# Holding operations behind transfers to program order from the third batch on, second buffers for q and k, and a sum as GpSimd's first library instruction

## The chip, the cores and the metric

The kernel runs on one core of a Trainium2 chip. The metric is the device time of one execution in microseconds (us); lower is better. A change within 0.2% (about 2.5 us) can't be told from no change.

## The reference, cut to what matters

```python
scores = scale * q @ k.T                                   # q, k, v: 8 batches, 8 heads, 576 x 64; scale = 1/8
bias   = -(cum[:, :, :, None] - cum[:, :, None, :])        # cum = cumsum of max(s, 0) along the 576
scores = where(causal, -1e9, scores + minimum(bias, 0))
attn   = exp(scores - max);  attn /= sum(attn) + 1e-9
x      = (attn @ v) with heads side by side                # 4608 tokens x 512
out    = (sigmoid(x @ w_gate) * (x @ w_val)) @ w_out       # w_gate, w_val: 512 x 1536, w_out: 1536 x 512
```

q, k and v are float32; the three weight matrices arrive as 64-bit floats and are decoded on the chip (`decode_weight`: three operations on VectorE and one on ScalarE for each block of 128 columns).

## The kernel before, in words

**Ticks.** 64 heads are gone through one after the other, each in five ticks: head `i`, tick `t` (0 to 4), `n = 5 i + t`. A tick takes one of five row blocks of the causal scores. The first eight heads (batch 0, functions `n_...`) work in float32; from head 8 on q, k, v and the probabilities are split into a high and a low half-precision part.

**What one head from head 8 on needs**, with the names that the profile uses:

- Every second head `load_qk` loads q and k of a pair of heads into `qk32` (queue SP), `qk_square` sums their squares (ScalarE, tile `jq`), a GpSimd all-reduce makes `qkt`, and `qk_scale` makes a power of two of it (`qksc`, `qkcf`; VectorE).
- `split_qk(i)`: two ScalarE operations write the high parts (L340, L342), two VectorE operations the low parts (L341, L343) into `qk16`, and one transposing transfer on SP (L345) turns it into the tile `T`. `swap_k(i)`: two more transfers on SP (L350, L351) copy the halves of k crosswise into `T[:, 2]`.
- `load_crow` fetches a row of cumulated biases from memory into `cr`, and GpSimd broadcasts it over the partitions. VectorE scales it to `rl`, GpSimd masks it (L403).
- `s_part(i, t)`: for each of six score pieces two matmuls on TensorE, the first (L388) against `T[:, 0]`, the second (L389) against the swapped copy `T[:, 2]`. Pieces are called `s46_4_0` (head 46, block 4, columns from 0), blocks go from 4 down to 0. `max_part` (L413, VectorE, tile `em`) adds bias and takes the maximum, ScalarE does the exponential (L416), `p_part` splits the probabilities (L420 ScalarE, L421 VectorE), a transposing transfer (`pt`) turns them, and two heads later `av_part` does 45 matmuls (L436 to L438).
- `v_square` loads a batch's v in four pieces on GpSimd's queue and sums squares on ScalarE for the batch after.

**FFN units.** 216 units (`gv`, 24 or 48 matmuls, L583; then `th` on ScalarE, `t` on VectorE, `h` on both; then six matmuls L613 into `o`) are dealt out over the ticks, each batch's units while the next batch is in attention; `m = n - 7` sets how far behind.

**What sets the order.** The code says what depends on what and a priority (the order in which it is written). A scheduler that goes by its own costs then fixes one order for each engine and each queue before the launch. On the chip every engine and every queue takes its instructions in that order, and one that waits holds up all behind it. `tc.keep_in_program_order(x)` places `x` behind everything that was written earlier for its engine.

**Buffers.** `qk32` and `qk16` have one buffer each, `T` two, `gv` (PSUM) two, the score banks three. The 24 tiles `t2f` (256 columns each) hold the first two FFN groups' results until the output weights are there; after tick 87 nothing uses them.

**GpSimd's sets of operations.** In GpSimd's order a row `ISA` without tiles (in the trace a `MODIFY_POOL_CONFIG`) stands where it is switched to another set of operations, called a library here; the profile of before has GpSimd idle behind both of them.

Of the kernel before, what the change touches and what calls it, by code (L numbers as in the profile page):

```python
# [7 lines left out]
F16 = mybir.dt.float16  # L8
# [15 lines left out]
def tile_attention_then_gated_ffn(  # L24
# [56 lines left out]
    for t, (q0, m, w) in enumerate(TILES):  # L81
# [7 lines left out]
    nc.gpsimd.memset(junk, 0.0)  # L89
    nc.gpsimd.affine_select(junk, junk, pattern=[[-1, P]], compare_op=ALU.is_ge, fill=0.0, base=0,  # L90
                            channel_multiplier=1)
    nc.vector.memset(ident, 0.0)
# [55 lines left out]
    sv = {}  # L148
    vss = {}

    def v_square(b, c):
        if c == 0:
            vss[b] = wp.tile([P, vch], F32, tag="vss", name=f"vss{b}")
        t = wp.tile([P, S], F32, tag="rl", name=f"vsq{b}_{c}")
        nc.gpsimd.dma_start(t, vview[b, c])
        nc.scalar.activation(t, t, AF.Square, accum_out=vss[b][:, c : c + 1])

# [49 lines left out]
    def load_weight(n):  # L207
# [3 lines left out]
        for x, src in enumerate((w_out,) if o else (w_gate, w_val)):  # L211
# [122 lines left out]
    def split_qk(i):  # L334
        p, j = divmod(i, 2)
        sc = qkc[p][0]
        t16 = wp.tile([QP, 2, QC, 2, D], F16, tag="qk16", name=f"qk16_{i}", bufs=1)
        q_ = qk32[p][:, 0, j]
        k_ = qk32[p][:, 1, j]
        nc.scalar.activation(t16[:, 1, :, 0], q_, AF.Copy, scale=sc[:QP, 0:1])  # L340
        nc.vector.scalar_tensor_tensor(t16[:, 1, :, 1], q_, sc[:QP, 0:1], t16[:, 1, :, 0], ALU.mult, ALU.subtract)  # L341
# [7 lines left out]
    def swap_k(i):  # L349
        nc.sync.dma_start(T[i][0:64, 2], T[i][64:128, 0])  # L350
        nc.sync.dma_start(T[i][64:128, 2], T[i][0:64, 0])  # L351

    def load_crow(i):
        crow[i] = wp.tile([P, S], F32, tag="cr", name=f"cr{i}")
        if i > 0:
            nc.sync.dma_start(crow[i][0:1], cum_d[i : i + 1, :])
        nc.gpsimd.partition_broadcast(crow[i], crow[i][0:1] if i > 0 else rel[0:1])  # L357

# [289 lines left out]
    nticks = NTL * NH  # L648
    for n in range(nticks + 8):
        i, t = divmod(n, NTL)  # L650
# [43 lines left out]
        if i < NH:  # L694
            p, j = divmod(i, 2)
            b, h = divmod(i, H)
            if t == 0 and i + 1 < NH:
                load_crow(i + 1)
            if i + 2 < NN:
                if j == 0 and t == 1:  # L700
                    n_load(p + 1)
                    load_v(p + 1)
                if j == 1 and t == 2:
                    with first():
                        n_prep(p + 1)
            elif i < NN:
                if j == 0:
                    if t == 2:
                        load_qk(p + 1)
                        load_v(p + 1)  # L710
                    if t == 4:
                        qk_square(p + 1)
            elif j == 0:
# [89 lines left out]
```

## Time and profile before

| | |
|---|---|
| three timed runs | 1224.86, 1225.04, 1225.22 us; median 1225.04 |
| the profiled execution | 1222.6 us; its span 1220.9 us |
| TensorE (PE) | busy 1114.0 us, 91% of the span |
| VectorE (DVE), ScalarE (ACT), GpSimd (POOL) | busy 783.0, 756.7, 299.4 us |
| granted TensorE clock, mean | 0.979 |

Busy is the time in which an engine had an instruction under way; matmuls overlap, so the share of PE is read as an upper bound. Rows of a timeline give start, duration, engine, line, tiles, and in brackets the idle time before with the instruction that ended it. SPq is the queue that SyncE feeds. A "lead" below is the PE work that stands between two instructions in the order. Head 18 begins at 273.7 us, head 63 at 1030.1 us.

### The profile page before, as it was taken

To read this page: it belongs to the slowest core of one execution; us is meant where nothing else is said; L and a number is where in the kernel's file an instruction comes from. 1 tells how busy PE (TensorE), PEld (TensorE's weight loads), DVE (VectorE), ACT (ScalarE), POOL (GpSimd) and SP (SyncE) were. 2 spreads that over 40 slices of the span, in tenths; PEclk is the share of its full clock that TensorE was granted. 3 is DMA by queue.
4 is the path that set the end of the run, shared out by engine and by line. 5 is a ranking of instruction groups with operands and counts; after the bars stand their busy time and mean duration, and the time that the engine had idled before them with its cause. 6 is when DMAs were issued, how large, how long until landed. Compare 5 with 4: busy or idle time off the path is not lost.

```text
span 1220.9 us, 30743 instructions
## 1 busy us (share of the span) xinstructions
PE 1114.0 (91%) x11924; PEld 871.3 (71%) x11924; DVE 783.0 (64%) x2194; ACT 756.7 (62%) x1505; POOL 299.4 (25%) x605
## 2 busy tenths in 40 slices
PE   2878687999999899999999999999999999999997
PEld 1666576667777777777777776777777777787774
DVE  4898997975777667764575566776677676422221
ACT  3988886766676667664665566676676676333222
POOL 2642543332232223221121122322232221000000
PEclk9976999999999999999999999999999999999999
DMA  8754798786786878783756477787888856300000
GB/s 226 213 154 133 173 199 169 150 162 130 153 153 135 152 135 155 157 164 70 130 113 128 80 151 150 149 145 158 149 156 143 168 103 122 55 19 10 10 18 18
DMA packets 464177, 157.51 MB, mean 129 GB/s; under 512 B 438495, under 2 KB 457951, under 8 KB 464030
## 3 DMA queue, kind: packets, MB, share of 16 engines
q1 hardware_dynamic: 444190, 117.79, 52.4%
q0 software_dynamic: 5440, 18.88, 5.0%
q10 hardware_dynamic: 14400, 18.88, 5.0%
q8 instruction: 93, 1.52, 0.5%
q14 instruction: 54, 0.44, 0.1%
HBM read 56.92 MB, written 9.58 MB: 54 GB/s over the span
## 4 chain that ended last, share of the span: by engine, by line
PE 34%; issue 24%; DMA 18%; DVE 9%; ACT 8%; POOL 4%; SPq 1%; POOLq 0%; ACTq 0%; DVEq 0%
PE gv L583 17%; DMA T<-qk 10%; PE o L613 9%; DMA qk<-in_q_dram 3%; DVE e L413 3%; DMA cr<-cum_d 2%; PE s L388 1%; PE na_ps L531 1%; ACT jq L313 1%; PE s L389 1%; PE s L502 1%; DMA vsq<-in_v_dram 1%; POOL cr L357 1%; ACT qk L340 1%; POOL rl L403 1%
## 5 line engine op out<-in xcount | busy, mean ns | idle before, releaser
L583 PE MATMUL gv<-x,w 128*128 128x256 f16 (+3 forms) x6912 | 618.7, 247 | 13.6 <-DVE t L590 9.9
L583 PEld LDWEIGHTS <-w 128*128 128x128 f16 x6912 | 536.2, 98 | 70.5 <-issue 15.9
L613 PE MATMUL o<-w2all,h 128*128 128x512 f16 x1296 | 314.1, 379 | 1.4 <-ACT osb L620 1.4
L403 POOL TENSOR_SCALAR_AFFINE_SELECT rl<-rl 128x64 f32<-128x64 f32 (+1 forms) x280 | 130.3, 466 | 380.1 <-DVE em L413 192.4
L416 ACT ACTIVATE e<-e,em 128x576 f32<-128x576 f32 x280 | 155.4, 557 | 75.3 <-DVE em L413 72.1
L613 PEld LDWEIGHTS <-h 128*128 128x128 f16 x1296 | 123.4, 98 | 108.8 <-issue 2.0
L590 DVE SCALAR_TENSOR_TENSOR t<-th,gv 128x256 f32<-128x256 f32 x192 | 80.0, 417 | 162.3 <-ACT th L588 162.2
L588 ACT ACTIVATE th<-gv,scb 128x256 f32<-128x256 f32 (+3 forms) x288 | 110.3, 408 | 114.9 <-PE gv L583 114.5
L598 ACT ACTIVATE h<-t,hsc 128x256 f16<-128x256 f32 x192 | 96.9, 505 | 92.0 <-DVE t L590 91.7
L421 DVE SCALAR_TENSOR_TENSOR p<-e,p 128x1152 f16<-128x1152 f32 x112 | 130.7, 1167 | 28.2 <-ACT p L420 27.6
L413 DVE CUSTOM_DVE_ANT_0 e<-s,rl,qkcf 128x288 f32<-128x288 f32 x280 | 134.5, 484 | 19.4 <-PE s L389 8.9
L599 DVE SCALAR_TENSOR_TENSOR h<-t,hsc,h 128x256 f16<-128x256 f32 x192 | 93.8, 488 | 41.3 <-ACT h L598 38.7
L420 ACT ACTIVATE p<-e 128x1152 f16<-128x1152 f32 x112 | 111.8, 998 | 3.7 <-DMA pt<-p 1.5
L388 PE MATMUL s<-T 128*128 128x288 f16 x336 | 86.7, 277 | 29.2 <-DVE em L413 25.8
L341 DVE SCALAR_TENSOR_TENSOR qk<-qk,qksc,qk 96x384 f16<-96x384 f32 x56 | 36.1, 645 | 87.9 <-ACT qk L340 87.8
L436 PE MATMUL av<-v,pt 128*128 128x65 f16 x840 | 84.5, 192 | 6.6 <-DMA pt<-p 6.4
L389 PE MATMUL s<-T 128*128 128x288 f16 x336 | 86.0, 277 | 3.4 <-DMA T<-T 3.4
L340 ACT ACTIVATE qk<-qk,qksc 96x384 f16<-96x384 f32 x56 | 34.3, 613 | 84.3 <-DMA T<-qk 83.8
L436 PEld LDWEIGHTS <-pt 128*128 128x128 f16 x840 | 77.2, 98 | 13.1 <-DMA pt<-p 7.7
L437 PE MATMUL av<-v,pt 128*128 128x64 f16 x840 | 84.4, 192 | 0.0
L438 PE MATMUL av<-v,pt 128*128 128x65 f16 x840 | 84.1, 194 | 0.0
L357 POOL PARTITION_BROADCAST cr<-cr x63 | 63.7, 1014 | 80.5 <-DMA cr<-cum_d 79.7
(149 smaller groups left out, 1305.0 us busy)
## 6 DMA issues: line engine op xcount, KB each, us to landing
vsq<-in_v_dram POOLq DMA_DIRECT2D x32, 288.0 KB, 4.1
out_dram<-osb POOLq DMA_DIRECT2D x36, 256.0 KB, 3.3
v<-in_v_dram SPq DMA_DIRECT2D x64, 128.0 KB
qk<-in_q_dram SPq DMA_DIRECT2D x28, 288.0 KB
qk<-in_k_dram SPq DMA_DIRECT2D x28, 288.0 KB
T<-T SPq DMA_DIRECT2D x112, 72.0 KB
ws<-in_moe_w_out_dram ACTq DMA_DIRECT2D x12, 512.0 KB
w2all<-in_moe_w_gate_dram ACTq DMA_DIRECT2D x8, 512.0 KB
```

The source lines that it names most:

```text
L388: nc.tensor.matmul(ps[:, : b_ - a], lhs, T[i][:, 0, a:b_], start=True, stop=False)
L389: nc.tensor.matmul(ps[:, : b_ - a], lhs, T[i][:, 2, a:b_], start=False, stop=True)
L403: nc.gpsimd.affine_select(rl[i][:, q0:w], rl[i][:, q0:w], pattern=[[-1, m]], compare_op=ALU.is_ge, fill=-MASKED if i < NN else MASKED, bas ...
L413: nc.vector.tensor_tensor_reduce(e_t[t][:, a:b_], ps[:, : b_ - a], rl[i][:, a:b_], c, init, ALU.add, ALU.min, acc)
L416: nc.scalar.activation(e_t[t][:, :w], e_t[t][:, :w], AF.Exp, bias=init, scale=-1.0)
L420: nc.scalar.activation(p_s[h_][:, 0], e_s[h_], AF.Copy, scale=PSCALE)
L421: nc.vector.scalar_tensor_tensor(p_s[h_][:, 1], e_s[h_], PSCALE, p_s[h_][:, 0], ALU.mult, ALU.subtract)
L436: nc.tensor.matmul(AV[i][:, t], hi, v_[:, D : 2 * D + 1], start=kb == 0, stop=False)
L583: nc.tensor.matmul(ps[:, gv, a:e], w1[f][:, cc, gv, wl], x_of(b, cc)[:, xl, c0 + a : c0 + e], start=(c == 0), stop=(c == 3 * NC - 1))
L588: nc.scalar.activation(th[:, a:e], ps[:, 0, a:e], AF.Tanh, scale=scb[b][:, f : f + 1])
L598: nc.scalar.activation(h[:, 0], t2, AF.Copy, scale=hsc[:, f : f + 1])
L613: nc.tensor.matmul(ps[:m], h[:, hl, tt * P : tt * P + m], w2[f][:, wl], start=(f == 0 and c == 0), stop=(f == NF - 1 and c == 2))
```

## The change

Six things, all in the order or the buffers; the arithmetic is the same.

1. GpSimd's first library instruction at the start, a mask on a scratch tile, becomes a sum over partitions.
2. The loads of weight blocks 0 and 1 go to the queue SP, written ahead of the first `cr` and v; block 2 stays on ScalarE's queue, held to program order.
3. From tick 90 (`more_room`; head 18) `spare` gives a second buffer for `qk32` (odd pairs) and for `qk16` (odd heads), both in the `t2f` tiles, now one tile.
4. From then on `pin` holds these behind all that is written before: the squares of q and k, `qk_scale`'s first operation, the first operation of `split_qk`, the two transfers of `swap_k`, the broadcast of `cr`, the sum of squares of v.
5. From then on they are written later: broadcast at tick 2 (was 0); q and k are loaded a pair of heads further ahead; squares at tick 0 of the odd head (was 4 of the even one), `qk_scale` at its tick 1 (was 0), `split_qk` of an even head at its tick 2 (was 1); `swap_k` of an even head at tick 4 (was 3). `v_square` loads a head earlier, the sum two ticks after its load.
6. From tick 110 on FFN units are dealt out nine ticks behind, not seven.

```diff
-    nc.gpsimd.affine_select(junk, junk, pattern=[[-1, P]], compare_op=ALU.is_ge, fill=0.0, base=0,
-                            channel_multiplier=1)
+    nc.gpsimd.partition_all_reduce(junk[:, 1:2], junk[:, 0:1], P, ADD_REDUCE)
...
+    def pin(ins):
+        return tc.keep_in_program_order(ins) if spare else ins
...
-    t2first = [cp.tile([P, GT], F32, name=f"t2f_{u}") for u in range(2 * NF)]
+    t2big = cp.tile([P, 2 * NF * GT], F32, name="t2f")
+    t2first = [t2big[:, u * GT : (u + 1) * GT] for u in range(2 * NF)]
+    spare = {}
+    def more_room():
+        c = 0
+        for name, n in (("qk16", QC * 2 * D), ("qk32", 4 * QC * D)):
+            spare[name] = t2big[:, c : c + n]
+            c += n
...
-            nc.scalar.dma_start(dst, src)
+            if n < 2:
+                nc.sync.dma_start(dst, src)
+            else:
+                d = nc.scalar.dma_start(dst, src)
+                if n == 2:
+                    tc.keep_in_program_order(d)
...
-        nc.scalar.activation(t16[:, 1, :, 0], q_, AF.Copy, scale=sc[:QP, 0:1])
+        pin(nc.scalar.activation(t16[:, 1, :, 0], q_, AF.Copy, scale=sc[:QP, 0:1]))
...
-        nc.sync.dma_start(T[i][0:64, 2], T[i][64:128, 0])
-        nc.sync.dma_start(T[i][64:128, 2], T[i][0:64, 0])
+        pin(nc.sync.dma_start(T[i][0:64, 2], T[i][64:128, 0]))
+        pin(nc.sync.dma_start(T[i][64:128, 2], T[i][0:64, 0]))
...
+            if t == (2 if spare else 0) and i + 1 < NH:
+                spread_crow(i + 1)
...
+                late = 1 if spare else 0
+                if t == 0 and p + 1 not in qkc:
                     qk_square(p + 1)
-            if NN - 1 <= i and j == 1 and i + 1 < NH:
-                if t == 0:
+                if t == late:
                     qk_scale(p + 1)
-                if t == 1:
+                if t == 1 + late:
                     split_qk(i + 1)
-            if t == 3 and NN - 1 <= i and i + 1 < NH:
+                if t == 3 and spare and i + 3 < NH:
+                    load_qk(p + 2)
+            if t == (3 + j if spare else 3) and NN - 1 <= i and i + 1 < NH:
                 swap_k(i + 1)
...
-        m = n - 7
+        m = n - (9 if n > 2 * NTL * H + 30 else 7)
```

How the order moves, at three places. First GpSimd's start, before (`ISA` without tiles: a library; `nq`: zeroed tiles of batch 0; `cr0`: the first broadcast):

```order
L362 MEMSET v32_0_168 64x130
L90 ISA
L90 AFFINE_SELECT scrap_89<-scrap_89 128x128
L479 MEMSET nq0_0_174 64x576
L479 MEMSET nq1_0_408 64x576
L479 MEMSET nq0_1_175 64x576
L479 MEMSET nq1_1_409 64x576
L362 MEMSET v32_1_261 64x130
L364 MEMSET v32_0_168 128x10
L357 ISA
L357 ISA cr0_166<-rel_121 128x576
```

The same place on GpSimd in the changed program:

```order
L394 MEMSET v32_0_149 64x130
L90 ISA
L90 ISA scrap_89<-scrap_89 128x1
L511 MEMSET nq0_0_155 64x576
L511 MEMSET nq1_0_385 64x576
L511 MEMSET nq0_1_156 64x576
L511 MEMSET nq1_1_386 64x576
L394 MEMSET v32_1_238 64x130
L396 MEMSET v32_0_149 128x10
L389 ISA cr0_147<-rel_121 128x576
```

One library row is left of two: none stands ahead of the first broadcast, and none ahead of the masks behind it.

Second VectorE at the split for head 46 (an even head; `t` and `h` are an FFN unit's, `em44_3` a maximum of head 44), before. Sixty rows stand between this split and the maximum `em46_4_0` that needs it:

```order
L421 SCALAR_TENSOR_TENSOR p16_0_81<-e_0_79,p16_0_81 128x768
L341 SCALAR_TENSOR_TENSOR qk16_46_12396<-qk32_23_12181,qksc23_12283,qk16_46_12396 96x6x64
L343 SCALAR_TENSOR_TENSOR qk16_46_12396<-qk32_23_12181,qksc23_12283,qk16_46_12396 96x6x64
L590 SCALAR_TENSOR_TENSOR t2_9_7_12050<-th9_7_12048,gv9_7_12023 128x256
L397 TENSOR_SCALAR rl45_12260<-cr45_12016,qkcf22_11772 128x576
L413 ISA e_1_80,em44_3_0_12178<-s44_3_0_12061,rl44_12002,qkcf22_11772 128x448
```

The same split on VectorE in the changed program, from the maximum `em45_1_0` on:

```order
L445 ISA e_0_79,em45_1_0_12431<-s45_1_0_12371,rl45_12175,qkcf22_11801 128x192
L445 ISA em45_1_0_12431 128x1
L622 SCALAR_TENSOR_TENSOR t2_9_10_12360<-th9_10_12358,gv9_10_12333 128x256
L354 TENSOR_SCALAR qksc23_12310<-qke23_12308 128x2
L356 SCALAR_TENSOR_TENSOR qkcf23_12312<-qksc23_12310 128x1
L357 SCALAR_TENSOR_TENSOR qkcf23_12312<-qksc23_12310 128x1
L429 TENSOR_SCALAR rl46_12436<-cr46_12189,qkcf23_12312 128x576
L358 RECIPROCAL qkcf23_12312<-qkcf23_12312 128x1
L631 SCALAR_TENSOR_TENSOR h9_10_12362<-t2_9_10_12360,hsc_112,h9_10_12362 128x256
L371 SCALAR_TENSOR_TENSOR qk16_46_12326<-t2f_135,qksc23_12310,qk16_46_12326 96x6x64
L373 SCALAR_TENSOR_TENSOR qk16_46_12326<-t2f_135,qksc23_12310,qk16_46_12326 96x6x64
```

The split for head 46 has moved from behind head 44's first exponential to behind the maximum of head 45's block 1; `em46_4_0` is now nine rows behind it.

Third the queue SP around head 46's `T`, before (`pt0_44`: probabilities; `qk32_24`: the next pair's q and k):

```order
L345 DMA_TRANSPOSE T46_12401<-qk16_46_12396 128x12x96
L350 DMA T46_12401<-T46_12401 64x576
L424 DMA_TRANSPOSE pt0_44_12332<-p16_0_81 128x12x128
L351 DMA T46_12401<-T46_12401 64x576
L303 DMA qk32_24_12704<-in_q_dram 96x12x64
```

The queue SP in the changed program:

```order
L456 DMA_TRANSPOSE pt1_45_12376<-p16_1_82 128x18x128
L386 DMA cr48_12719<-cum_d_114 1x576
L375 DMA_TRANSPOSE T46_12331<-qk16_46_12326 128x12x96
L330 DMA t2f_135<-in_k_dram 96x12x64
L380 DMA T46_12331<-T46_12331 64x576
L381 DMA T46_12331<-T46_12331 64x576
L456 DMA_TRANSPOSE pt0_45_12503<-p16_0_81 128x12x128
```

`T46` now stands behind head 45's first probabilities (it stood ahead of head 44's second), and its two swaps follow each other.

On TensorE the two halves of a score piece, next to each other before, are apart now. Between the end of `s45_1` and head 46 stand, in the changed order: unit `gv9_11` (24 matmuls) and six matmuls `o`, `s45_0`, three `o`, `gv10_0` (24), three `o`, ten matmuls of `av44`; then the first halves of `s46_4_0`, `s46_4_288` and `s46_3_0`, then 26 matmuls of `av44`, then their second halves. Of the 22 even heads from 20 to 62, eleven (20, 22, 36 to 48, 60, 62) have, like this one, no more than 34 matmuls of `av` or 14 of `gv` between their first and second halves; the other eleven have half an FFN unit or more there, and most of them (24 to 34) have their split up to a block earlier and less work ahead of the first halves. Odd heads have half a unit or more between their halves, or a whole one or more ahead of the first.

More of the change, by code (lines that the diff above doesn't have):

```diff
@@ L148, in tile_attention_then_gated_ffn @@
     sv = {}
-    vss = {}
+    vss, vsq = {}, {}
     def v_square(b, c):
@@ L155, in v_square, with v_square_sum @@
         nc.gpsimd.dma_start(t, vview[b, c])
-        nc.scalar.activation(t, t, AF.Square, accum_out=vss[b][:, c : c + 1])
+        if b == 0:
+            nc.scalar.activation(t, t, AF.Square, accum_out=vss[b][:, c : c + 1])
+        else:
+            vsq[b, c] = t
+    def v_square_sum(b, c):
+        t = vsq.pop((b, c))
+        pin(nc.scalar.activation(t, t, AF.Square, accum_out=vss[b][:, c : c + 1]))
     def v_scale(b):
@@ L281, in weight_step @@
         n = wnext["step"]
-        while wnext["load"] < len(wsteps) and room(wnext["load"])[2] < n:
+        while n and wnext["load"] < len(wsteps) and room(wnext["load"])[2] < n:
             load_weight(wnext["load"])
@@ L300, in load_qk @@
         b, h0 = divmod(2 * p, H)
-        t = wp.tile([QP, 2, 2, QC, D], F32, tag="qk32", name=f"qk32_{p}", bufs=1)
+        if spare and p % 2:
+            t = spare["qk32"][:QP].rearrange("p (i h c d) -> p i h c d", i=2, h=2, d=D)
+        else:
+            t = wp.tile([QP, 2, 2, QC, D], F32, tag="qk32", name=f"qk32_{p}", bufs=1)
         for i, src in enumerate((q, k)):
@@ L320, in qk_scale @@
         e0 = wp.tile([P, 2], I32, tag="qk0", name=f"qk0_{p}")
-        nc.vector.tensor_scalar(e0, qkc[p].bitcast(I32), 23, None, ALU.logical_shift_right)
+        pin(nc.vector.tensor_scalar(e0, qkc[p].bitcast(I32), 23, None, ALU.logical_shift_right))
         e1 = wp.tile([P, 2], F32, tag="qk1", name=f"qk1_{p}")
@@ L336, in split_qk @@
         sc = qkc[p][0]
-        t16 = wp.tile([QP, 2, QC, 2, D], F16, tag="qk16", name=f"qk16_{i}", bufs=1)
+        if spare and i % 2:
+            t16 = spare["qk16"][:QP].bitcast(F16).rearrange("p (a c l d) -> p a c l d", a=2, l=2, d=D)
+        else:
+            t16 = wp.tile([QP, 2, QC, 2, D], F16, tag="qk16", name=f"qk16_{i}", bufs=1)
         q_ = qk32[p][:, 0, j]
         k_ = qk32[p][:, 1, j]
-        nc.scalar.activation(t16[:, 1, :, 0], q_, AF.Copy, scale=sc[:QP, 0:1])
+        pin(nc.scalar.activation(t16[:, 1, :, 0], q_, AF.Copy, scale=sc[:QP, 0:1]))
         nc.vector.scalar_tensor_tensor(t16[:, 1, :, 1], q_, sc[:QP, 0:1], t16[:, 1, :, 0], ALU.mult, ALU.subtract)
@@ L356, in load_crow, with spread_crow @@
             nc.sync.dma_start(crow[i][0:1], cum_d[i : i + 1, :])
-        nc.gpsimd.partition_broadcast(crow[i], crow[i][0:1] if i > 0 else rel[0:1])
+    def spread_crow(i):
+        pin(nc.gpsimd.partition_broadcast(crow[i], crow[i][0:1] if i > 0 else rel[0:1]))
     def load_v(p):
@@ L640, in tile_attention_then_gated_ffn @@
     n_load(0)
+    for wnext["load"] in range(2):
+        load_weight(wnext["load"])
+    wnext["load"] = 2
     load_crow(0)
+    spread_crow(0)
     load_v(0)
@@ L648, in tile_attention_then_gated_ffn @@
     nticks = NTL * NH
-    for n in range(nticks + 8):
+    for n in range(nticks + 12):
+        if n == NOFF + 3:
+            more_room()
         i, t = divmod(n, NTL)
@@ L705, in tile_attention_then_gated_ffn @@
                         n_prep(p + 1)
-            elif i < NN:
-                if j == 0:
-                    if t == 2:
+            elif j == 0 and i + 2 < NH:
+                if t == 2:
+                    if p + 1 not in qk32:
                         load_qk(p + 1)
[L710 to L713, printed above, removed]
+                    load_v(p + 1)
+                if t == 4 and not spare:
+                    qk_square(p + 1)
+            if NN <= i and j == 0:
                 if t == 0:
@@ L735, in tile_attention_then_gated_ffn @@
             if b + 1 < B:
-                if t == 3 and 2 <= h < 2 + vch:
-                    v_square(b + 1, h - 2)
-                if t == 4 and h == 6:
+                if t == 2 and 1 <= h < 1 + vch:
+                    v_square(b + 1, h - 1)
+                if t == 4 and 1 <= h < 1 + vch:
+                    v_square_sum(b + 1, h - 1)
+                if t == 1 and h == 6:
                     v_scale(b + 1)
```

10 lines of the change are left out of this document (4 added, 6 removed).

## The prediction

> **What bounds the kernel now.** I read the head of the page, busy time by stage, the groups on PE and the waits of the long middle stage, then the timelines of the start and of heads 44 to 46.
>
> ```profile
> span 1220.9 us, 30743 instructions
> PE 1114.0 (91%) x11924; PEld 871.3 (71%) x11924; DVE 783.0 (64%) x2194; ACT 756.7 (62%) x1505; POOL 299.4 (25%) x605
> ...
> 0.00:28.00 28.00, 6.14 (x18) 3.71 (x18) 10.31 (x19) 7.91 (x12) 7.50 (x29) 1.00 0.82 230
> 28.00:130.00 102.00, 83.06 (x461) 68.15 (x462) 87.81 (x255) 91.55 (x192) 45.37 (x79) 0.83 0.59 169
> 130.00:274.00 144.00, 119.69 (x1233) 93.61 (x1233) 122.88 (x367) 107.15 (x214) 59.24 (x102) 0.98 0.84 169
> 274.00:1040.00 766.00, 732.54 (x8552) 573.74 (x8551) 518.57 (x1457) 498.29 (x977) 182.20 (x385) 1.00 0.72 138
> 1040.00:1221.00 181.00, 172.56 (x1664) 132.06 (x1662) 43.45 (x101) 51.83 (x111) 5.08 (x10) 0.99 0.09 22
> ```
>
> A stage's row gives the stretch, its length, then PE, PEld, DVE, ACT and POOL busy, the granted clock and the transfers. PE is the bound, and what can be won is its idle time: 21.9 us in the first 28 us, 18.9 up to 130, 24.3 up to 274, 33.5 while heads 18 to 63 run, 8.4 in the last stage. The pins, the second buffers and the longer lag act in the fourth stage alone, so they share 33.5 us. From 28 to 130 us ACT is busy 91.55 of 102 us: there ACT and DVE bound.
>
> What ends PE's idle time in the fourth stage, from the groups and the waits of that stretch:
>
> ```profile
> L583 PE MATMUL gv<-x,w 128*128 128x256 f16 (+3 forms) x4992 | 426.0, 243 | 13.0 <-DVE t L590 9.9 <-DMA x<-x 3.0
> L388 PE MATMUL s<-T 128*128 128x288 f16 (+4 forms) x272 | 69.8, 277 | 20.1 <-DVE em L413 18.0 <-DMA v<-in_v_dram 1.8
> ...
> ACT qk L340 <- DMA T<-qk: 78.0, 37, 4.6
> ```
>
> 27.9 of the 33.5 us come from DVE being late (`em` 18.0, `t` 9.9). And ACT stood 78.0 us, 2.1 us in each of 37 heads, because the one `qk16` buffer was still being turned into `T`; every exponential and `th` behind it stood too. Head 47's split shows it:
>
> ```profile
> 754.44 1.30 SPq L345 DMA_TRANSPOSE T<-qk  x1
> 759.70 0.47 SPq L350 DMA_DIRECT2D T<-T  x1
> ...
> 759.71 0.61 ACT L340 ACTIVATE qk<-qk,qksc 96x384 f16<-96x384 f32 x1 [2.13 <-DMA T<-qk]
> ...
> 760.36 0.61 DVE L341 SCALAR_TENSOR_TENSOR qk<-qk,qksc,qk 96x384 f16<-96x384 f32 x1 [2.72 <-ACT qk L340]
> 760.89 0.61 DVE L343 SCALAR_TENSOR_TENSOR qk<-qk,qksc,qk 96x384 f16<-96x384 f32 x1
> ...
> 761.89 0.52 DVE L397 TENSOR_SCALAR rl<-cr,qkcf 128x576 f32<-128x576 f32 x1
> ```
>
> **The start.** Before, two libraries are loaded, one ahead of the scratch mask, one ahead of the first broadcast:
>
> ```profile
> 13.69 0.28 POOL L90 TENSOR_SCALAR_AFFINE_SELECT scrap<-scrap 128x128 f32<-128x128 f32 x1 [11.49 <-issue]
> 14.03 2.76 POOL L479 MEMSET nq<- 64x576 f32 x4
> ...
> 24.93 0.86 POOL L357 PARTITION_BROADCAST cr<-rel  x1 [7.73 <-issue]
> ...
> 26.58 0.30 POOL L403 TENSOR_SCALAR_AFFINE_SELECT cr<-cr 128x128 f32<-128x128 f32 x1
> ...
> 28.56 0.45 DVE L511 CUSTOM_DVE_ANT_0 e<-s,cr 128x288 f32<-128x288 f32 x1
> ...
> 29.07 2.07 PE L502 MATMUL s<-nk,nq 128*128 128x320 f32 x4 [8.33 <-DVE em L511]
> ```
>
> In the changed order the second load is gone, so the first mask comes 7.7 us earlier; the first maximum no longer stands behind a weight decode that waits for GpSimd, 28.56 - 26.58 = 2.0 us more. Upper bound 9.7 us. Against it: the decode of weight blocks 0 and 1, which filled DVE and ACT while POOL loaded, now comes behind head 0's maxima, and those engines bound the next 100 us. Of the 10.3 and 7.9 us that they were busy before 28 us most is that decode; if about half moves out, 5.2 and 4.0 us are paid back, which leaves 4.5 to 5.7. I take -5, bounds -9.7 and +2 (all of the decode late). The weights' way over SP costs nothing there: q and k stand ahead of them on SP, and the v and `cr` loads behind them are wanted by PE and POOL only after the library (11.5 us for the first at worst). The sum itself (one small operation) runs where the mask of 0.28 us ran.
>
> **Between 28 and 274 us** no pin is in force; v's squares for batch 1 come one head earlier, the same four on ACT. I take 0, bounds -5 and +5, a fifth of the 24.3 us that PE idles from 130 to 274, since the scheduler has put the whole stretch in another order.
>
> **Taken away from head 18 on.** With a second `qk16`, ACT's 78.0 us of standing have no cause left, and DVE's `em` and `t` behind it come earlier. 9.9 and 18.0 us of PE's idle time hang on them; the 3.0 for `x` and 1.8 for v do not. I take four fifths, -22, bounds -14 (half: the rest would be DVE's own queue) and -27.9. Broadcast and squares a tick or two later, and q and k loaded ahead, cost nothing: POOL is busy 182 of 766 us, and the split waits for DVE and ACT, not for them. The longer lag puts two ticks of FFN work into the last stage, where PE is busy up to its last matmul: it is moved, not added, 0.
>
> **Added: `T` comes just in time.** Before, head 46's `T` was issued at 754.44 and first read at 768.72, 14.3 us later:
>
> ```profile
> 750.19 0.25 PE L389 MATMUL s<-T 128*128 128x192 f16 x1
> ...
> 759.03 0.19 PE L436 MATMUL av<-v,pt 128*128 128x65 f16 x1
> ...
> 760.40 2.78 PE L583 MATMUL gv<-x,w 128*128 128x256 f16 x24
> 763.02 1.46 PE L613 MATMUL o<-w2all,h 128*128 128x512 f16 x6
> 764.31 0.30 PE L388 MATMUL s<-T 128*128 128x320 f16 x1
> ...
> 768.66 0.19 PE L388 MATMUL s<-T 128*128 128x64 f16 x1
> ...
> 768.72 0.29 PE L388 MATMUL s<-T 128*128 128x288 f16 x1
> 768.85 0.29 PE L389 MATMUL s<-T 128*128 128x288 f16 x1
> ```
>
> These starts give PE's pace: a unit of 24 matmuls 2.62 us, six `o` 1.29, one `av` (760.40 - 759.03) / 45 = 0.030, a first half 0.13. In the changed order PE has, from the end of `s45_1` to the first halves of head 46, 2.62 + 1.29 + 0.06 + 0.65 + 2.62 + 0.65 + 0.30 = 8.2 us of work; to the second halves 0.46 + 26 x 0.030 = 1.25 more, 9.4. Against that stand, from the same `s45_1`, its drain (0.25) and DVE's rows up to the end of the split, then the transfers. DVE first:
>
> ```profile
> 750.73 0.42 DVE L590 SCALAR_TENSOR_TENSOR t<-th,gv 128x256 f32<-128x256 f32 x1
> ...
> 751.72 0.54 DVE L599 SCALAR_TENSOR_TENSOR h<-t,hsc,h 128x256 f16<-128x256 f32 x1
> 752.18 0.41 DVE L413 CUSTOM_DVE_ANT_0 e<-s,rl,qkcf 128x192 f32<-128x192 f32 x1
> 752.51 0.08 DVE L413 DVE_READ_ACCUMULATOR2_ANT em<- 128x1 f32 x1
> ```
>
> `em` 0.41, its read-out and four small ones at 0.08 to 0.16 each, `t` 0.42, `rl` 0.52, `h` 0.54, the split 0.61 + 0.61: 3.5 to 3.8 us, and 3.1 where the next starts before the last ends, as the two of the split do (0.53 apart). The transfers, from rows of the chain of waits:
>
> ```profile
> 392.71 3.31 DMA T<-qk
> ...
> 408.39 6.71 DMA T<-qk
> ...
> 754.44 5.24 DMA T<-qk
> ...
> 228.29 2.75 DMA T<-T
> ```
>
> Those on the chain lie between 3.31 and 6.71; it picks out the late ones, so I take 4.2 in the mean. A swap took 2.75; the second goes out 0.5 behind the first. So `T` is there 0.25 + 3.3 + 0.1 + 4.2 = 7.9 us after `s45_1`, its swapped part at 7.9 + 0.5 + 2.75 = 11.1: the first halves find it with 0.3 us to spare, the second halves are 1.7 late. PE waits for that with all FFN work queued behind. Counted in the same way the eleven even heads built like this one are 0.2 to 2.1 late; of the eleven others four (24, 26, 32, 34) are about 1.5 late at their first halves and the rest on time. That is 1.7 at the worst third and nothing at another third: 0.7 per even head, times 22, +15. Bounds: 0 (transfers at their shortest, 3.31 and about 2) and 2.2 x 22 = +48 (DVE's full durations at every head). Odd heads have enough work between their halves.
>
> **Sum**: -5 + 0 - 22 + 15 = -12. The profiled execution took 1222.6 us, 2.4 below the median of the timed runs; 1222.6 - 12 = 1210.6, so 1213 against the median of 1225.0.
>
> **Rivals.**
>
> *`T` never late.* If the transfers land as the short ones do, -5 - 28 = -33: 1192. For it: the chain's durations are of transfers that shared the queue with others, and the changed order sends the swaps back to back. Against: of those on the chain none is under 3.31. The Trainium skill (DMA: Bandwidth & Descriptors, "Anatomy of one DMA") puts the fixed cost of a transfer at about 2 us, mostly the receipt at its end; by that as the whole price the two in a row are done in about 4 us and this rival wins, and the trace's 3.31 to 6.71 for the transposing one speaks against it.
>
> *DVE late as well (slower).* The count lets DVE take up the block's maximum as soon as its matmul is done. The trace has it later: matmul 750.19 + 0.25, maximum 752.18, 1.7 us. Part of that is ACT's wait, which goes; if 1.0 stays, each even head is 1.7 late, 22 x 1.7 = 37, and -5 - 22 + 37 = +10: 1235. It decides from 27 / 22 = 1.2 us per even head on. For it: the split now has nine rows to head 46's maximum, where it had sixty, and nothing else that PE could do stands ahead. Against: a wait of PE lets DVE catch up before the next.
>
> *No change.* With 1.1 to 1.3 us per even head the gain at the start and the second buffers are eaten up: 1225.
>
> *The start gains nothing*, if the moved decode costs what the load gave: 1218, still faster. The order speaks against a reload, since no library row is left behind the first.
>
> **How the numbers follow.** The forecast (gains of 2.5 to 20 us) gets 0.43, `T` never late 0.14, no change within 0.2% (2.5 us, about what a measurement can tell) 0.14, DVE late 0.29. Faster 0.57, same 0.14, slower 0.29. The forecast's own range is 1205 to 1222. The range for 8 in 10 goes down into the first rival and up just past the second: 1196 to 1238. The full bounds, -9.7 - 5 - 27.9 + 0 and +2 + 5 - 14 + 48, would be 1182 and 1266.
>
> **What the changed profile would show.** Right: on POOL one long idle stretch at the start, the first maximum before 22 us; no ACT wait for `T<-qk` after head 20; PE's idle time from head 18 on 25 to 28 us, with waits for `T<-T` or `T<-qk` of 10 to 20 us among it and less than 8 behind `em` and `t`. Wrong: waits for `T` above 27 us, or PE's idle time behind `em` and `t` as long as before; at the start, a second gap on POOL of over 5 us.

## The result, and the profile after

The changed kernel took 1241.7 us (median of four runs, 1237.8 to 1248.5) against 1225.1 for the kernel before: ratio 1.0141, interval 1.0109 to 1.0173, 1.4% slower. Forecast were 1213 us and a gain. The profiled execution of the changed kernel took 1237.8 us, 15.2 more than that of the kernel before.

The head of the page and the busy time by stage, after (columns as before: PE, PEld, DVE, ACT, POOL busy, granted clock, transfers' share, GB/s):

```profile
span 1236.0 us, 30675 instructions
PE 1121.7 (91%) x11924; PEld 870.4 (70%) x11924; DVE 785.8 (64%) x2194; ACT 747.1 (60%) x1505; POOL 302.9 (25%) x605
...
0.00:28.00 28.00, 18.61 (x88) 13.99 (x88) 17.98 (x43) 18.15 (x36) 14.75 (x40) 0.94 0.96 272
28.00:130.00 102.00, 79.72 (x485) 61.94 (x485) 91.85 (x273) 91.78 (x195) 52.95 (x93) 0.86 0.65 180
130.00:274.00 144.00, 126.31 (x1248) 93.81 (x1247) 116.59 (x341) 102.81 (x205) 46.29 (x82) 0.97 0.83 171
274.00:1040.00 766.00, 709.57 (x8300) 557.54 (x8298) 507.52 (x1421) 473.83 (x947) 182.12 (x378) 0.98 0.70 132
1040.00:1236.00 196.00, 187.48 (x1811) 143.18 (x1809) 51.86 (x120) 60.52 (x126) 6.79 (x14) 0.99 0.11 27
```

Length minus PE's busy time is its idle time: 9.4, 22.3, 17.7, 56.4 and 8.5 us, against 21.9, 18.9, 24.3, 33.5 and 8.4 before. Up to 274 us PE idles 15.7 us less, in the fourth stage 23.0 more, in all 7.4 more. Its busy time rose by 7.7 for the same matmuls. 7.4 + 7.7 = 15.1, the whole difference of the spans. The clock in the first row is no reading, here or before: the profile has no record of it until 39.6 us in the kernel before and until 13.4 us in the changed one. Until then a 128x288 float32 matmul takes 0.69 us in both, against 0.41 later at full clock.

What ends PE's idle time in the fourth stage, after: the waits of that stretch (total, times, longest), then the page's groups of the second and first halves of the score pieces:

```profile
PE s L421 <- DMA T<-T: 43.9, 25, 5.8
PE s L420 <- DMA T<-qk: 11.9, 12, 2.7
PE s L420 <- DVE em L445: 0.5, 1, 0.5
...
L421 PE MATMUL s<-T 128*128 128x288 f16 x336 | 81.2, 288 | 48.1 <-DMA T<-T 48.1
...
L420 PE MATMUL s<-T 128*128 128x288 f16 x336 | 82.4, 280 | 24.4 <-DMA T<-qk 19.5
```

The 27.9 us behind VectorE's `em` and `t` are gone but for 0.5, and ScalarE's 78.0 us of waiting for `T<-qk` are gone. In their place stand 55.8 us of waiting for `T`: 11.9 for the transposing transfer, 43.9 for the swap. By heads, 30.6 us of this fall on even heads (21 of 22 wait, 1.4 each, at most 3.2) and 25.2 on ten odd heads (six of them 2.9 to 5.8). Before, PE didn't wait for `T` in this stretch. The sign named for a wrong forecast, waits for `T` above 27 us, has come.

Two heads show how. Head 46, the prediction's example, in the timeline of the changed kernel:

```profile
759.54 1.36 DVE L453 SCALAR_TENSOR_TENSOR p<-e,p 128x1152 f16<-128x1152 f32 x1
759.57 0.25 PE L421 MATMUL s<-T 128*128 128x192 f16 x1
...
760.89 0.41 DVE L445 CUSTOM_DVE_ANT_0 e<-s,rl,qkcf 128x192 f32<-128x192 f32 x1
...
761.37 2.70 SPq L456 DMA_TRANSPOSE pt<-p  x1
...
763.41 0.60 DVE L373 SCALAR_TENSOR_TENSOR qk<-t2f,qksc,qk 96x384 f16<-96x384 f32 x1
...
764.65 1.25 SPq L375 DMA_TRANSPOSE T<-qk  x1
...
768.07 0.49 SPq L380 DMA_DIRECT2D T<-T  x1
...
771.97 1.01 PE L421 MATMUL s<-T 128*128 128x288 f16 x3 [2.48 <-DMA T<-T]
```

Block 1 of head 45 ends at 759.82. VectorE, busy with a split of probabilities until 760.90, takes the block's maximum 1.1 us later. The split for head 46 ends at 764.01, but queue SP is held by the transposing transfer of head 45's probabilities until 764.07 and then issues a `cr` row, so `T` goes out at 764.65. The swap goes out at 768.07, and PE, which has run dry, gets it at 771.97. Head 33, an odd one:

```profile
503.89 1.28 SPq L375 DMA_TRANSPOSE T<-t2f  x1
...
506.83 6.24 SPq L456 DMA_TRANSPOSE pt<-p  x1
...
513.17 0.54 SPq L380 DMA_DIRECT2D T<-T  x1
...
514.45 5.27 SPq L456 DMA_TRANSPOSE pt<-p  x1
...
521.04 1.03 PE L421 MATMUL s<-T 128*128 128x288 f16 x3 [5.79 <-DMA T<-T]
```

Here `T` is there in time, but the swap stands on queue SP behind the transposing transfer of the probabilities, which holds the queue for 6.24 us; the swap goes out 9.3 us after `T`, and PE has the copy 7.9 us after that, with other transfers on the way.

The start, from the timeline, after: POOL's sum, its first broadcast and mask, and the first maximum.

```profile
2.28 0.39 POOL L90 PARTITION_ALL_REDUCE scrap<-scrap  x1
...
7.82 0.86 POOL L389 PARTITION_BROADCAST cr<-rel  x1
...
9.29 0.30 POOL L435 TENSOR_SCALAR_AFFINE_SELECT cr<-cr 128x128 f32<-128x128 f32 x1
9.72 0.46 DVE L543 CUSTOM_DVE_ANT_0 e<-s,cr 128x288 f32<-128x288 f32 x1 [3.32 <-POOL cr L435]
```

Both of the earlier stops of POOL are gone, the one of 11.49 us ahead of the scratch mask as well as the one of 7.73 ahead of the broadcast. The first maximum runs at 9.72 instead of 28.56.

### The profile page after: what moved, and what is told of

Read it like the earlier page. It is cut to its first block, busy times and chain, and to the rows that moved or that the text cites. A ratio compares the mean times of both kernels' runs of the same rounds, so it can differ in the third digit from the quotient of the medians.

```text
span 1236.0 us, 30675 instructions
## 1 busy us (share of the span) xinstructions
PE 1121.7 (91%) x11924; PEld 870.4 (70%) x11924; DVE 785.8 (64%) x2194; ACT 747.1 (60%) x1505; POOL 302.9 (25%) x605
## 4 chain that ended last, share of the span: by engine, by line
PE 38%; issue 22%; DMA 16%; DVE 10%; ACT 6%; SPq 3%; POOL 2%; ACTq 0%; POOLq 0%; DVEq 0%
PE gv L615 20%; PE o L645 10%; DMA T<-T 8%; DMA T<-qk 6%; PE s L421 3%; DVE e L445 2%; PE s L420 2%; SPq L456 1%; SPq L380 1%; DVE p L453 1%; PE av L470 1%; PE av L468 1%; PE av L469 1%; ACT p L452 1%; ACT w L276 1%
## 5 line engine op out<-in xcount | busy, mean ns | idle before, releaser
L615 PE MATMUL gv<-x,w 128*128 128x256 f16 (+3 forms) x6912 | 635.0, 248 | 4.0 <-DVE t2f L622 4.0
L645 PE MATMUL o<-w2all,h 128*128 128x512 f16 x1296 | 320.0, 383 | 0.0
L421 PE MATMUL s<-T 128*128 128x288 f16 x336 | 81.2, 288 | 48.1 <-DMA T<-T 48.1
L420 PE MATMUL s<-T 128*128 128x288 f16 x336 | 82.4, 280 | 24.4 <-DMA T<-qk 19.5
L468 PE MATMUL av<-v,pt 128*128 128x65 f16 x840 | 88.8, 193 | 4.3 <-DMA pt<-p 4.1
L469 PE MATMUL av<-v,pt 128*128 128x64 f16 x840 | 88.6, 193 | 0.0
L470 PE MATMUL av<-v,pt 128*128 128x65 f16 x840 | 88.4, 195 | 0.0
L468 PEld LDWEIGHTS <-pt 128*128 128x128 f16 x840 | 77.9, 98 | 12.2 <-DMA pt<-p 5.5
L469 PEld LDWEIGHTS <-pt 128*128 128x128 f16 x840 | 77.7, 97 | 7.0 <-issue 0.2
L421 PEld LDWEIGHTS <-T 128*128 128x128 f16 x336 | 30.7, 100 | 71.7 <-DMA T<-T 53.3
L470 PEld LDWEIGHTS <-pt 128*128 128x128 f16 x840 | 77.7, 97 | 2.4 <-issue 0.2
```

What stands on the lines that cost most here:

```text
L421: nc.tensor.matmul(ps[:, : b_ - a], lhs, T[i][:, 2, a:b_], start=False, stop=True)
L468: nc.tensor.matmul(AV[i][:, t], hi, v_[:, D : 2 * D + 1], start=kb == 0, stop=False)
L469: nc.tensor.matmul(AV[i][:, t, 0:D], hi, v_[:, 0:D], start=False, stop=False)
L470: nc.tensor.matmul(AV[i][:, t], lo, v_[:, D : 2 * D + 1], start=False, stop=kb == t)
L615: nc.tensor.matmul(ps[:, gv, a:e], w1[f][:, cc, gv, wl], x_of(b, cc)[:, xl, c0 + a : c0 + e], start=(c == 0), stop=(c == 3 * NC - 1))
L645: nc.tensor.matmul(ps[:m], h[:, hl, tt * P : tt * P + m], w2[f][:, wl], start=(f == 0 and c == 0), stop=(f == NF - 1 and c == 2))
```

## The experiments

Each row of the table is a kernel on the chip, with its ratio to the kernel before on the same chip; "T" is PE's waiting for `T` and "idle" all of PE's idle time, both from 274 to 1040 us of the profiled execution. These two columns are of one execution each, while timed runs of one kernel lie up to some 1.7% apart (e6: 1222.4 to 1243.4 us), so a few us between two rows of them say little.

| kernel | median us | ratio (interval) | T | idle |
|---|---|---|---|---|
| changed kernel | 1241.7 | 1.0141 (1.0109 to 1.0173) | 55.8 | 56.4 |
| e1 sum alone | 1212.1 | 0.9894 (0.9857 to 0.9932) | 0 | 32.9 |
| e2 early parts alone | 1222.9 | 0.9982 (0.9956 to 1.0009) | 0 | 41.6 |
| e3 no pins | 1211.5 | 0.9904 (0.9874 to 0.9934) | 0 | 30.2 |
| e4 pins, a tick earlier | 1253.6 | 1.0226 (1.0163 to 1.0289) | 58.7 | 61.6 |
| e5 swap not pinned | 1235.5 | 1.0103 (1.0077 to 1.0130) | 47.6 | 48.0 |
| e6 split not pinned | 1231.1 | 1.0068 (1.0029 to 1.0107) | 47.2 | 47.4 |
| e7 no pins, lag 7 | 1230.5 | 1.0055 (1.0020 to 1.0089) | 0 | 47.9 |
| e8 sum, second buffers | 1222.3 | 0.9990 (0.9965 to 1.0015) | 0 | 37.7 |
| e9 split, swap, scale not pinned | 1200.3 | 0.9829 (0.9782 to 0.9876) | 15.6 | 26.5 |
| e10 all pins, lag 7 | 1226.8 | 1.0004 (0.9967 to 1.0041) | 44.9 | 45.8 |
| e11 sum, lag 9 | 1204.2 | 0.9848 (0.9817 to 0.9880) | 0 | 28.2 |
| e12 sum, buffers, lag 9 | 1207.8 | 0.9881 (0.9847 to 0.9916) | 0 | 26.6 |
| e13 e2 with v as before | 1215.2 | 0.9947 (0.9918 to 0.9976) | 0 | 34.3 |
| e14 e9 with v as before | 1206.5 | 0.9881 (0.9846 to 0.9916) | 14.6 | 26.8 |
| e15 e9 with lag 7 | 1193.1 | 0.9750 (0.9681 to 0.9819) | 2.2 | 16.1 |

**e1: the sum alone**, on the kernel before.

```diff
-    nc.gpsimd.affine_select(junk, junk, ...)
+    nc.gpsimd.partition_all_reduce(junk[:, 1:2], junk[:, 0:1], P, ADD_REDUCE)
```

> The kernel before with one edit: GpSimd's first library instruction is the sum. Theory (the gain at the start comes from the library that is not loaded a second time): PE's idle time in the first 28 us falls by 8 to 12 us, no second gap on POOL, the run 7 to 12 us faster, 1213 to 1218. Rival (the gain of 15.7 us of PE idle time up to 274 us comes from the weight loads on queue SP and from the new order as a whole): the sum alone gives less than 5 us, 1220 or more.

1.06% faster (0.7 to 1.4), some 13 us. PE idles 15.9 us up to 28 us instead of 21.9, and 52.2 instead of 65.1 up to 274. The sum by itself carries the gain at the start. The time came out just past the theory's 7 to 12 us; PE's idle time in the first 28 us fell by 6.0 us and not by 8 to 12, and the rest of the 12.9 lies between 28 and 274 us. From its timeline:

```profile
2.27 0.39 POOL L90 PARTITION_ALL_REDUCE scrap<-scrap  x1
...
9.54 0.85 POOL L356 PARTITION_BROADCAST cr<-rel  x1
```

**e2: the early parts alone** (the changed kernel without `more_room()`, and with lag 7; this leaves out the second buffers, every `pin` and the later ticks of q, k and the broadcast, while v's earlier load and later sum, the weights on queue SP and the held load of block 2 stay).

> The changed kernel without its fourth-stage parts: no second buffers, no pins, no later ticks, lag 7; what is left acts before 274 us. Theory (the change gains before head 18 and loses behind it): PE idle up to 274 us about 49 us as in the changed kernel, the fourth stage as before with 30 to 36 us idle, the run 1207 to 1214. Rival (head 18 begins only 2.2 us earlier in the changed kernel, so the early gain is only work moved, paid back later): 1220 to 1226.

No different from the kernel before that the interval could tell. The early gain is there (53.4 us idle up to 274), but the fourth stage idles 41.6 us instead of 33.5, 19.6 behind `em` and 17.0 behind `t`. My theory fell, and the rival has the time: what was gained early isn't kept. What costs it in the fourth stage is looked for in e13.

**e3: no pins.** `pin` gives back its argument; buffers, later ticks and lag 9 stay.

> The changed kernel with nothing held to program order from head 18 on; the second buffers, the later ticks and lag 9 stay. Theory (the pins set how late T comes, because the scheduler left free puts the split earlier): waits of PE for T fall from 55 us to under 20 us, 1192 to 1208. Rival (the later ticks alone make T late): waits for T of 40 us or more, 1230 to 1245.

The theory holds: not one wait for `T`, 0.96% faster than the kernel before, though no faster than the sum alone. `T` goes out 14.5 us (even heads) and 14.3 us (odd) ahead of its first matmul in the median, much as before (14.5 and 13.5); in the changed kernel it is 4.0 and 5.0. The waits of PE in its fourth stage, and ScalarE's for the `qk16` buffers:

```profile
PE gv L615 <- DMA x<-x: 13.9, 4, 5.8
PE s L420 <- DVE em L445: 12.6, 8, 2.9
...
ACT t2f L370 <- DMA T<-t2f: 48.7, 20, 4.8
ACT qk L370 <- DMA T<-qk: 17.2, 9, 3.5
```

The last two rows were not expected: with a second `qk16` and no pins ScalarE still stands 65.9 us for it. I take it that the free scheduler uses the room to split further ahead and stands in front of the next buffer instead; for heads 35 to 42 `T` goes out 22 us or more ahead.

**e4: a tick earlier**, pins in force.

```diff
-                late = 1 if spare else 0
+                late = 0
...
-            if t == (3 + j if spare else 3) and ...
+            if t == 3 and ...
```

> The changed kernel with the scale, the split and the swap of an even head written a tick earlier again (split at tick 1, swap at tick 3 of the odd head); pins, second buffers and lag 9 stay. A tick is about 3.3 us. Theory (T is late by 0 to 3 us at an even head because it is written a tick later): even heads' waits nearly vanish, odd heads' stay (in the changed trace about 20 us of the 55), waits for T 15 to 25 us in all, 1200 to 1212. Rival (pins make T late whatever the tick): 1232 or more.

It was slower still, with 58.7 us of waits for `T`, as the rival said. My theory of the tick was wrong: the even heads, whose split is a tick earlier, wait 49.9 us instead of 30.6, the odd ones 8.8 instead of 25.2. At tick 1 of an odd head the program has just written `x_part` and `split_x`, and a pinned split stands behind those: in 18 of 44 splits, all for even heads, ScalarE's row ahead is `x<-xq` (L486), in the changed kernel in none of 45. A place earlier in the program isn't an earlier time when the work written just ahead of it is itself late.

**e5 and e6: one pin taken away**, the swap's or the split's.

```diff
-        pin(nc.sync.dma_start(T[i][0:64, 2], T[i][64:128, 0]))     # e5, both swaps
+        nc.sync.dma_start(T[i][0:64, 2], T[i][64:128, 0])
...
-        pin(nc.scalar.activation(t16[:, 1, :, 0], q_, ...))        # e6
+        nc.scalar.activation(t16[:, 1, :, 0], q_, ...)
```

> The changed kernel with the two transfers of the swap no longer held to program order; all other pins stay. Theory (the pin on the split's first operation makes T late: ScalarE can't split before the exponentials written ahead of it, and these wait for the matmuls that PE does last before it runs dry): waits of PE for T stay at 40 us or more, 1230 to 1245. Rival (the swap's place behind the transposing transfer of the probabilities on queue SP is the cause, 43.9 of the 55.9 us being waits for the swap): waits for T below 20 us, 1205 to 1218.

> The changed kernel with the split's first operation no longer held to program order; the swaps and all else stay held. Theory (the split's pin is the cause): T goes out 10 us or more ahead of its first matmul instead of 4 to 5, waits for T below 15 us, 1205 to 1220. Rival (the swap's pin): T goes out early and PE still waits for the swap, 30 us or more, 1225 to 1240.

PE's waits of the fourth stage, first e5, then e6:

```profile
PE s L421 <- DMA T<-T: 32.4, 24, 3.3
PE s L420 <- DMA T<-qk: 15.2, 13, 2.9
```

```profile
PE s L421 <- DMA T<-T: 27.4, 23, 2.3
PE s L420 <- DMA T<-qk: 19.8, 12, 5.7
```

Neither pin alone is the cause; taking one away removes about 8 of 55.8 us. e5 came out as its theory forecast; that theory, the split's pin alone, fell in e6, where the rival's forecast came true. In e5 odd heads' swaps follow `T` after 3.1 us (7.0 in the changed kernel) and their waits fall from 25.2 to 11.7, while even heads' rise from 30.6 to 35.9. In e6 odd heads' `T` goes out 14.4 us ahead, but their swap is still held; they wait 13.4, and even heads, whose `T` is as late as ever, 33.8. I take it that the pin on `qk_scale` ahead of it still holds their split; it was taken away in e9 together with the other two, never alone.

**e9: all three pins on `T`'s way taken away**; squares, broadcast and v's sum stay pinned.

```diff
-        pin(nc.vector.tensor_scalar(e0, qkc[p].bitcast(I32), 23, None, ALU.logical_shift_right))
+        nc.vector.tensor_scalar(e0, qkc[p].bitcast(I32), 23, None, ALU.logical_shift_right)
```

(and those of e5 and e6)

> The changed kernel with three pins gone (split, swap, qk_scale's first operation); the squares of q and k, the broadcast and the sum for v stay held. Theory (every pin on T's way holds it; in the order the split of an even head now stands 10 to 24 VectorE rows ahead of the maximum that needs it, against 8 to 26 in the changed kernel and 18 to 44 without any pin): waits for T fall from 55.9 to 5 to 25 us, 1210 to 1228. Rival (split, scale and swap are all of it): no wait for T, 1205 to 1215.

```profile
PE s L421 <- DMA T<-T: 10.9, 9, 3.0
PE gv L615 <- DMA x<-x: 10.6, 4, 3.7
PE s L420 <- DMA T<-qk: 4.7, 5, 1.6
```

1.7% faster than the kernel before, below the bottom of the forecast of its theory, whose waits for `T` of 5 to 25 us came: they fall to 15.6 us, 0.6 of it at odd heads. `em` and `t` don't come back, and no wait of ScalarE for `qk16` is left. I take it that the squares, still pinned, keep the split from running as far ahead as in e3; no run separates that.

**e7, e10, e11, e12, e15: the lag.** One line, 7 or 9, with no pins, with all pins, without buffers, with buffers and no pins, with e9's pins.

> The changed kernel without pins and with FFN units dealt out seven ticks behind, as before; second buffers and later ticks stay. Without pins at lag 9 it took 1211.5. Theory (the lag only moves work): 1207 to 1216. Rival (the longer lag gives PE work to cover with): 1218 or more, with PE waits behind VectorE in place of it.

> The changed kernel, all pins in force, with FFN units dealt out seven ticks behind as before. Without pins lag 7 took 1230.5 against 1211.5 at lag 9. Theory (the longer lag itself gains, since a unit's matmuls then find x finished, and the pins lose beside it): waits for T as in the changed kernel, waits for x and VectorE added, 1245 to 1262. Rival (the longer lag is what makes ScalarE's queue late, through units written ahead of the pinned split): waits for T fall below 40 us, 1222 to 1235.

> The kernel before with the sum as GpSimd's first library instruction (1212.1 alone) and lag 9 from tick 110 on. Theory (lag 9 gains by itself): PE's 29 us behind VectorE fall to about 15, 1195 to 1205. Rival (lag 9 only helps where the second buffers let ScalarE run on; or it only puts the scheduler's order another way): 1208 to 1218.

> The kernel before with the sum, second buffers for qk32 and qk16, and lag 9; no pins, no later ticks, v's pieces as before. With lag 7 it took 1222.3. Theory (lag 9 is worth 10 to 19 us once the buffers are there): 1203 to 1213. Rival (lag is worth nothing, the 19 us between two unpinned kernels were the scheduler's other order): 1217 to 1226.

> The kernel with the three pins on T's way gone (1200.3 at lag 9) at lag 7. Theory (the longer lag gains wherever T isn't the wait, and costs where it is): 1207 to 1222. Rival (lag 9 costs wherever anything is pinned): 1185 to 1198.

Lag 9 gains 1.5% without pins (e7 to e3) and 1.1% with sum and buffers (e8 to e12); with the sum alone (e1 to e11) the gain of 0.5% isn't separated by the intervals. With all pins it costs 1.4% (e10 to the changed kernel), and with e9's pins the medians say that it costs 0.8%, with intervals that overlap. So three of my theories fell: in e7 (the lag is not just moved work), in e10 (its rival has the time, though the waits for `T` of 44.9 us are above the 40 that it asked for) and in e15, whose rival came true; those of e11 and e12 came out in time. PE's waits in e10, then its fourth stage and waits in e15:

```profile
PE s L421 <- DMA T<-T: 34.0, 27, 3.5
PE s L420 <- DMA T<-qk: 10.9, 13, 1.6
```

```profile
274.00:1040.00 766.00, 749.88 (x8843) 593.61 (x8841) 528.99 (x1474) 503.08 (x984) 185.44 (x387) 1.00 0.72 138
...
PE gv L615 <- DMA x<-x: 13.5, 5, 3.5
PE s L420 <- DMA T<-t2f: 1.7, 1, 1.7
PE s L421 <- DMA T<-T: 0.5, 1, 0.5
```

In both pinned pairs two ticks of lag go with 11 to 13 us more waiting for `T` (44.9 to 55.8, 2.2 to 15.6). Why is not settled: the lag shifts which FFN units are written ahead of a pinned split, and no run isolates that. Nor does any run tell a gain of the lag itself from that of the other order that the scheduler makes after every edit. By its median e15 is the fastest kernel, 2.5% (1.8 to 3.2) below the kernel before, and its interval is clear of that of the sum alone; it overlaps e9's, and just that of e11, which has neither pins nor second buffers.

**e8: sum and second buffers, free order, lag 7.**

> The kernel before with the sum as GpSimd's first library instruction (1212.1 alone) and second buffers for qk32 and qk16 from tick 90, nothing else. Theory (ScalarE's 77 us of waiting for the one qk16 buffer caused most of the 28 us that PE idles behind VectorE): ScalarE's wait goes, PE's idle time from head 18 on falls from 33 to 10 to 18 us, 1190 to 1203. Rival (VectorE is late by its own queue, and ScalarE's wait cost nothing): idle time stays at 28 us or more, 1208 to 1216.

Nothing is gained over the sum alone and some 1% lost. The rival's idle time of 28 us or more came (37.7), at a time above its range too. ScalarE's wait, which should have gone, is still there, so the run doesn't say what would happen without it:

```profile
ACT t2f L354 <- DMA T<-t2f: 46.9, 19, 5.0
ACT qk L354 <- DMA T<-qk: 25.0, 9, 4.7
```

**e13 and e14: v's pieces** loaded and squared as before, in e2 and in e9.

> The kernel of the early parts alone (1222.9) with v's pieces loaded and squared as before; left of the change are the sum, the weight blocks 0 and 1 on queue SP and block 2 held to program order. Theory (v's pieces, loaded a head earlier and squared two ticks later, hold one of the two buffers that the rows rl need and make VectorE late): 1208 to 1215, as with the sum alone. Rival (the weights on queue SP, or only another order): 1219 to 1226.

> The kernel with the three pins on T's way gone (1200.3), with v's pieces loaded and squared as before. Theory (v's pieces cost up to 10 us wherever they are): 1190 to 1197. Rival (they cost only where the order is free, or nothing): 1198 to 1208.

e13 is 0.5% faster than the kernel before, just past the upper end of its theory's range (1215), and idles 34.3 us in the fourth stage instead of e2's 41.6. That speaks for v's pieces as e2's loss, but the two intervals just overlap. In e14 the same edit gains nothing, as the rival said, so v's pieces aren't a fixed cost; I take it that the order around them decides.

## Why the prediction was wrong, step by step

**"`T` comes just in time", +15: the step that failed.** It measured 55.8 us. Its two halves failed in different ways. For even heads the worked example was near (1.7 late forecast at head 46, 2.5 measured), but "0.7 per even head", a mean with nothing at a third of them, was not: 21 of 22 waited, 1.4 us in the mean.

What the count left out is in the example's rows: `T` goes out 5.1 us after `s45_1` begins, where I counted 3.65. VectorE takes the block's maximum 1.1 us after its matmul and not at once, and queue SP adds half a us between the end of the split and `T`. The transposing transfer was faster than I took it (the swap goes out 3.4 us after `T`, not 4.2), and the swap slower (3.9 us from the first of its two issues, not 0.5 + 2.75). These errors cancel in part, so that the example came out near is luck in part. The late maximum is the rival "DVE late as well", which let 1.0 us stay and asked 1.7 per even head. My reason against it, that PE's wait lets DVE catch up, did not hold. Why it did not is argued here and not shown: a pinned split waits, through ScalarE's rows ahead of it, for matmuls that PE does late before it runs dry, and the next head begins the same chain again. An exponential is ScalarE's row ahead of 39 of 45 splits, but it is in e3 too, at 37 of 44, where no `T` is late; so it matters which exponential it is. The delays of the other even heads aren't broken down.

For odd heads I put 0 ("enough work between their halves"), having read the order on queue SP for an even head alone; 25.2 us were lost there. That the chain of pins is the cause is shown by e3, e5, e6 and e9 (0, 47.6, 47.2 and 15.6 us of waits for `T`), and at lag 7 by e10 and e15 (44.9 and 2.2); the pin on `qk_scale` was not taken away alone.

**The start, -5: right sign, too small.** PE idles 12.5 us less in the first 28 us of the trace, and the sum alone makes the run 13 us faster in e1. With the other early parts the gain doesn't last: e2 keeps none of it that the interval could tell, e13 0.5%. The bound of -9.7 was wrong too: I let the library load that stays cost its 11.5 us, and in the trace no stop of POOL is left, so that one was charged to the mask and not to libraries in general. The sign named, one long idle stretch of POOL, did not come; the first maximum before 22 us did, at 9.72.

**Taken away, -22: right in size, up to its bound.** 27.9 us became 0.5, and in e15, where `T` is hardly waited for, `em` costs 0.4. That ScalarE's wait was the cause is not shown: in e11, at lag 9, it is 91.1 us with the one `qk16`, and PE idles only 17.5 behind `em` and `t`; in e1 it is 76.8, and PE idles 29.3. And "with a second `qk16` ACT's 78.0 us have no cause left" holds only in the pinned order: in e3 and e8 ScalarE still waits 65.9 and 71.9 us. The wait is gone only in the kernels with both second buffers and pins.

**Between 28 and 274 us, 0: right.** 40.0 us idle there against 43.2.

**The longer lag, 0: wrong.** Where the intervals tell it, it is worth 1.1 to 1.5% either way: a gain in the two pairs of kernels with second buffers and no pins, a loss with all pins.

**PE's busy time: a step that was missing.** The matmuls are the same, and PE is busy 7.7 us longer. From 274 to 1040 us the granted clock stood at half in two stretches before and in five after. Before, both; after, that behind head 33's wait and that around head 46's:

```profile
418.40:421.80 3.40, 3.40 (x36) 3.40 (x34) 3.37 (x7) 1.38 (x4) 0.48 (x1) 0.51 0.18 36
739.30:742.70 3.40, 3.40 (x19) 2.42 (x17) 2.80 (x12) 2.27 (x5) 1.03 (x2) 0.50 1.03 203
```

```profile
518.60:525.40 6.80, 4.36 (x15) 2.22 (x16) 2.58 (x8) 1.98 (x4) 1.42 (x3) 0.50 1.15 229
771.20:778.00 6.80, 6.03 (x34) 4.35 (x35) 3.50 (x11) 3.06 (x4) 2.28 (x4) 0.50 0.34 66
```

The stretches sum to 6.8 us before and 27.2 after. PE is busy in 6.8 and 22.8 us of them, at half speed a loss of 3.4 and 11.4: the 8.0 us between them are about the 7.7 that PE is busy longer. A wait for `T` of some length is paid a second time in clock.

**Rivals.** "`T` never late" put 1192 on a kernel of these buffers without the wait. e15 is such a kernel, with three pins fewer and lag 7, and took 1193.1; that the times agree so well is luck in part, since the start gave more than -5 and 13.5 us of waits for `x` came. The 2 us that this rival quotes from the Trainium skill (DMA: Bandwidth & Descriptors, "Anatomy of one DMA") are fitted there to transfers issued by GpSimd. Those of `T` are issued by SyncE, and no run here shows 2 us for them. "DVE late as well" had the sign and, for even heads, the mechanism, at 1235 and a chance of 0.29. Its even heads' waits were somewhat too large (37 us against 30.6); it had neither the 25.2 us of the odd heads nor the clock's 7.7, and its start gained too little.

## What to carry to other kernels

An instruction that is pinned to program order inherits the lateness of everything written ahead of it, and a chain of pins is only as early as the latest of them: freeing the split's or the swap's pin alone took away 8 us of waits, freeing these two and `qk_scale`'s 40. Before counting a just-in-time transfer as hidden, take the median lead from issue to first use for every case of the loop (here even and odd heads), count the queue in front of it, and let each hand-over between engines cost what it does in the trace. A second buffer need not take the producer's wait away (78.0 us before, 71.9 in e8) if the scheduler is free to give the producer another place.

## What the runs showed of the hardware

Half-clock stretches of TensorE came in lengths of 3.4 and 6.8 us and followed idle gaps. In the 17 profiles of this study, from 274 us on, 22 of 23 gaps above 3.4 us, 39 of 67 between 2 and 3.4, and 14 of 227 from 0.6 to 1.5 had such a stretch begin in the gap or within 3.5 us of its end. The Trainium skill (TensorE: Matmul & The Clock Gate, "HAM oscillation — how this bites in real kernels") gives as its rule no idle gaps of PE above about 3.4 us. The trace agrees above that length, but for one gap of 3.47 us in e15, and is stricter below it: the gap of 2.48 us that ends at 771.97 lies at a stretch at half clock, while one of 3.20 us that ends at 387.01 has the full clock behind it.

As far as these traces tell, what decides is not the length of a gap but how busy PE is in a fixed window, by the profile's busy time. The clock records of each profile change on a fixed grid of 3.41 us. From 274 to 1040 us, of the windows of this grid at full clock all 67 in which PE was busy for less than 41% were followed by a window at half clock, none of 3616 above 49%, and 6 of 24 between. After a window at half clock, all 73 with PE busy above 80% were followed by full clock, all 18 below 77% by half again. The gap of 3.20 us falls on two windows, which stay 52% and 54% busy; that of 2.48 us leaves its window 49% busy, and the next, at half clock, 76%:

```profile
387.01 0.61 PE L421 MATMUL s<-T 128*128 128x288 f16 x3 [3.20 <-DMA T<-T]
...
382.03:385.45 3.42, 1.78 (x16) 1.35 (x14) 2.05 (x8) 1.45 (x3) 0.00 (x0) 1.00 1.71 168
385.45:388.86 3.41, 1.85 (x14) 1.39 (x15) 1.11 (x4) 0.22 (x1) 0.12 (x1) 1.00 0.80 178
767.74:771.15 3.41, 1.66 (x38) 1.27 (x34) 0.76 (x2) 0.51 (x1) 0.00 (x0) 1.00 0.54 122
771.15:774.57 3.42, 2.60 (x19) 1.93 (x20) 1.54 (x7) 0.31 (x1) 0.28 (x2) 0.50 0.61 115
```

The Trainium skill's same page ("What's actually happening") says that the window is 3413 ns long and runs freely, without starting anew with the kernel; the traces agree with the length.

GpSimd began with a sum in the changed kernel and in e1 and showed no stop for a library, where beginning with a mask cost 11.5 us, and 7.7 more at the first broadcast.
